# Where the expert units of the first batch begin: ahead of, or behind, the routing of its first part

## The chip, the cores and the metric

The kernel runs on one core of a Trainium2 chip. A core has a matrix engine (PE, TensorE), a vector engine (DVE, VectorE), a scalar engine (ACT, ScalarE), GpSimd (POOL) and a sync engine (SP) that issues most transfers. The metric is the time of one execution in device microseconds, and the median over runs counts.

## The reference

Four sequences of 10048 tokens with 128 channels go through an attention over 49 agents, and then through a two-level mixture of experts. Cut to what matters:

```
a2k   = softmax(scale * agents @ k.T)      # 49 x 10048, for each batch
agent_v = a2k @ v                          # 49 x 128
x     = softmax(scale * q @ agents.T) @ agent_v
g     = argmax(x @ w_group)                # 4 groups
e     = argmax(x @ w_expert[g])            # 4 experts in each
out   = p_g * p_e * (relu(x @ w1[g, e]) @ w2[g, e])
```

Every token goes to one of 16 experts (128 to 1024 to 128 channels), and its row is scaled by the two probabilities.

## The kernel before

The batches are taken in the order SEQ = (1, 2, 3, 0). For each of the first three, one expert is chosen (the one that most of its first tokens want), and all its tokens go through that expert; what belongs to others is counted and would be done at the end. The last batch is sorted by expert. A number in 32 bits is carried as a high and a low half in 16 bits (xh, xl; hh, hl), so most products on PE come in two or three matmuls.

Tokens go in tiles of 512 (20 for each batch). An own tile has 8 units: `first` (L1270) multiplies the tile's transposed weights et with 128 columns of the expert's weights wbuf into a PSUM tile ph, of which there are three, ACT makes hh from it and DVE hl (`evicted`, L1263); `second` (L1282) multiplies hh and hl with w2 into po, eight units behind (LAG). At the eighth unit of a tile `out_rows` scales po by oo and writes it out; oo is read by `factors` (L1314) from cwt, where `weigh` has written the tokens' weights.

All other work of a batch lies in lanes, generators that emit a few instructions at each step: q0 to q3 (queries: load, scores, exponentials, split into halves), k1 to k3 (keys and values, up to the agents' vectors), a0 to a3 (`followed`, L680: logits, routing, weights), p3 (sorting). A batch's lane a goes in parts of a few tiles; `skewed` (L284) runs stage two of a part beside stage one of the next. After each unit `advance` (L1479) steps lanes that are behind their due share (QUEUE), as long as a budget for DVE and ACT lasts, and an a lane at most twice. A step that yields a number of units rests for so long. `own_tile` (L1507) and `run_second` (L1519) step lanes until what they need is there: et and the weights, or the tokens' weights for the tile whose eighth unit is second in line.

What the program emits is a priority; the instructions of each engine are laid out when the kernel is compiled, in an order in which one whose inputs are there may come before one that was emitted earlier. On the chip each engine goes through its own queue in that order.

The opening (L1551 to L1568) does the keys, the values and the first queries of the first batch by itself. `agents_done` ends with the choice of the expert (`choose_first`, L590) and the loads of its w1 and w2, and steps q0 three times at each of its own. `part_logits` makes the logits of part one (tiles 0 and 1). `part_weights` (L803) then has three things for part one: `expert_split` at high priority (the product of the first weights with the agents' vectors, the split of w1 and w2 into halves), `routing` (L866), and `weigh` (L906) with the write of cwt. At its first yield the opening runs 14 rounds over q0, k1 and a0 (L1565 to L1568). Only behind all that come the units. While `wide` is on, that is in the opening, PSUM tiles of lanes are taken from all eight banks, afterwards from three.

Of the kernel before, what the change touches and what calls it, by code (L numbers as in the profile page):

```python
# [11 lines left out]
F16 = mybir.dt.float16  # L12
# [22 lines left out]
TQ = TS // P  # L35
# [24 lines left out]
SEQ = (1, 2, 3, 0)  # L60
NOWN = B - 1
SORTED = SEQ[NOWN]
# [3 lines left out]
PARTS = ((0, 2), (2, 5), *SORTS[1:])  # L66
ST = 5 * TQ
# [9 lines left out]
AHEAD_TURNS = 2  # L77
HOP = 2
LANDING = 7
OPENING = (3, 14)  # L80
LAG = 8
GROUP = 4
STRIP = P // GROUP
# [58 lines left out]
def build(ctx, tc, qT, kT, v, agT, wr, w1, w2, cpk, out, cols):  # L142
# [28 lines left out]
    def bank(any_=True):  # L171

        if wide[0] and any_:
            turns[0] += 1
            k = turns[0] % 8
            if k in (0, 3, 6):
                return ps1.tile([P, TS], F32, name="ph")
            if k in (1, 4):
                return ps2.tile([P, TQ, C], F32, name="po").rearrange("p a c -> p (a c)")
        return psa.tile([P, 512], F32, name="at", tag="at")  # L180
# [43 lines left out]
    wbuf = [const.tile([P, 2 * F], I32, name=f"wbuf{i}") for i in range(NB)]  # L224
# [9 lines left out]
    state = {b: {} for b in range(B)}  # L234
# [49 lines left out]
    def skewed(n, *stages):  # L284

        for i in range(n + len(stages) - 1):
            yield "chunk"
            live = [[stages[k](i - k), 0] for k in reversed(range(len(stages))) if 0 <= i - k < n]
            while live:
                moved = False  # L290
                for x in list(live):
                    if x[1] > clock[0] and not forced[0]:
                        continue
                    y = next(x[0], "end")
                    if y == 0:
                        continue
                    moved = True
                    if y == "end":
                        live.remove(x)
                        continue  # L300
                    if isinstance(y, int):
                        x[1] = clock[0] + y
                    yield
                if not moved:
                    yield 0
# [374 lines left out]
    def followed(b):  # L680

        parts = PARTS if b == SEQ[0] else SORTS
        first_part = 1 if b == SEQ[0] else 0
        moved = lambda f: lambda k: f(b, *parts[k + first_part])
        yield from skewed(len(parts) - first_part, *[moved(f) for f in ((part_logits, part_positions, part_rows) if b == SORTED else (part_logits, part_weights))])
        if b == SORTED:
            yield from order(b)

# [79 lines left out]
    def turned(b, i):  # L768

        n = min(TQ, NT - i * TQ)  # L770
        while b != SORTED and sum(len(state[o].get("et", {})) for o in SEQ[:NOWN]) >= ETB - 2:
            yield 0
        ptr = bank().bitcast(F16)
        r = i * TQ // ST
        for q in range(n):
            pe.transpose(ptr[0:2 * NA, q * P:(q + 1) * P], state[b]["rows", r][:, i * TQ + q - r * ST, 0:2 * NA], ident)
        et = ep.tile([2 * NA, TS], F16, name="es", bufs=2) if b == SORTED else ep.tile([2 * NA, TS], F16, name="et")
        act.activation(et[:, 0:n * P], ptr[0:2 * NA, 0:n * P], AF.Copy)
        state[b].setdefault("et", {})[i] = et
        state[b].setdefault("turned", set()).add(i)  # L780
        state[b].setdefault("all", {})[i] = et
        yield

    def ends(i0, i1):
        return i0 * TQ, NTP if i1 == OT else i1 * TQ

    def have(b, i):
        return ("split", (min(NT, (i + 1) * TQ) - 1) // CT) in state[b]

    def part_logits(b, i0, i1):  # L790

        st = state[b]
        for i in range(i0, i1):
            while not have(b, i):
                yield 0
            if b != SORTED and i not in st.setdefault("turned", set()):
                yield from turned(b, i)
        while "rh" not in st:
            yield 0
        yield HOP  # L800
        yield from logits(b, *ends(i0, i1))

    def part_weights(b, i0, i1):  # L803

        st = state[b]
        if "expert" in st and i0 == 0:
            st["weights"] = wbuf[SEQ.index(b)].bitcast(F16)
            with tc.high_priority():
                for _ in expert_split(b, st.pop("expert"), st["weights"]):
                    pass  # L810
            st["ready"] = True
            yield from routing(b, *ends(i0, i1))
            cnt = rt.tile([P, NE], F32, name=f"cnt{b}")
            vec.tensor_reduce(out=cnt, in_=st["oh"], axis=AX.X, op=ALU.add)
            st["cnts"] = [cnt]
        else:
            yield from routing(b, *ends(i0, i1))
            if i0 == 0:
                yield from choose(b)
                st["ready"] = True  # L820
        yield from weigh(b, *ends(i0, i1))
        yield
        st["weighed"] = i1
        yield from kept(b, *ends(i0, i1))
# [12 lines left out]
    def logits(b, t0, t1):  # L837

        st = state[b]
        NL = NG + NE + 1  # L840
        r0 = t0 // ST * ST
        if t0 == r0:
            st["lg", r0 // ST] = pc.tile([P, NL, ST], F32, name="lg")
            if NTP <= r0 + ST:
                vec.memset(st["lg", r0 // ST][:, :, NT - r0:], 1.0)
        z = min(NT, t1)
        i0, i1 = t0 // TQ, -(-z // TQ)
        if b == SORTED:
            yield from turned(b, i0)
        pl = bank()  # L850
        for i in range(i0, i1):
            if b == SORTED and i + 1 < i1:
                yield from turned(b, i + 1)
            elif b == SORTED:
                yield HOP
            et = st["all"].pop(i)
            for t in range(i * TQ, min((i + 1) * TQ, z)):
                o = pl[:, (t - t0) * NL:(t - t0 + 1) * NL]
                for h in range(2):
                    pe.matmul(o, et[:, (t - i * TQ) * P:(t - i * TQ + 1) * P], st["rh"][:, h], start=(h == 0), stop=(h == 1))  # L860
            yield HOP if i + 1 == i1 else None
        plv = pl[:, 0:(z - t0) * NL].rearrange("p (t g) -> p t g", g=NL)
        act.activation(st["lg", r0 // ST][:, :, t0 - r0:z - r0].rearrange("p g t -> p t g"), plv, AF.Copy)
        yield HOP
# [313 lines left out]
    def expert_split(b, x, ws):  # L1178

        w1f, w2f = x["w"]  # L1180
        for h in range(2):
            ps = bank()
            s = slice(h * 512, (h + 1) * 512)
            pe.matmul(ps, state[b]["at"], w1f[:, s], start=True, stop=True)
            yield HOP
            act.activation(ws[:, s], ps, AF.Copy)
            vec.tensor_sub(out=ws[:, F + h * 512:F + (h + 1) * 512], in0=ps, in1=ws[:, s])
            yield
        wv = ws[:, 2 * F:].rearrange("p (k h c) -> p k h c", k=FB, h=2)
        tc.keep_in_program_order(act.activation(wv[:, :, 0], w2f, AF.Copy, scale=W2S))  # L1190
        yield
        for h in range(2):
            z = slice(h * FB // 2, (h + 1) * FB // 2)
            vec.scalar_tensor_tensor(out=wv[:, z, 1], in0=w2f[:, z], scalar=W2S, in1=wv[:, z, 0], op0=ALU.mult, op1=ALU.subtract)
            yield
# [13 lines left out]
    def load_ahead(*which):  # L1209
        for x in which:  # L1210
            loaded[x] = load(*x)
# [292 lines left out]
    def lane(name):  # L1504
        return next(y for y in lanes if y["name"] == name)
# [39 lines left out]
    def along(n, *names):  # L1545
        clock[0] += 1
        for y in [lane(x) for x in names for _ in range(n)]:
            if y["until"] <= clock[0]:
                step(y)

    A = SEQ[0]  # L1551
    with tc.tile_pool(name="early", bufs=1) as early:
        qe = early_queries(A)
        for _ in front(A, early, ORDER, qe):
            pass
        for _ in qe:
            pass
        load_ahead(*[("q", A, 1 + i) for i in range(KA)], ("k", SEQ[1], 0))
        for _ in agents_done(A, early):
            along(OPENING[0], "q0")  # L1560
        for _ in part_logits(A, *PARTS[0]):
            clock[0] += 1
        resting = True
        for _ in part_weights(A, *PARTS[0]):
            if resting and "weights" in state[A]:  # L1565
                resting = False
                for _ in range(OPENING[1]):
                    along(1, "q0", "k1", "a0")  # L1568
    mo = ctx.enter_context(tc.tile_pool(name="mo", bufs=2))
    wide[0] = False  # L1570

# [88 lines left out]
```

## Time and profile before

| | |
|---|---|
| median of 3 runs | 937.5 us (936.94 to 937.96) |
| profiled execution | 937.08 us, its span 935.0 us |
| busy share of the span | PE 92%, DVE 80%, ACT 66%, POOL 50% |
| mean granted clock of PE | 0.974 of 2.4 GHz |

The span goes from the first to the last instruction of the profiled execution. A busy share is an average over stages that have different limits. The chain that ended last is followed back from the last instruction to whatever released each step; its shares say where the time of the whole was set. Instructions in the trace bear the line of a helper (L137 stands for nearly all of PE, DVE and ACT), so they are told apart by the tiles that they write and read. The granted clock is 0.5 when PE is held at 1.2 GHz and 1.0 at 2.4 GHz.

### The profile page before, as it was taken

How to read it: one execution, taken by the hardware profiler on the slowest of the kernel's cores; microseconds unless marked ns; L12 is line 12 of the kernel's file. 1: busy time of each engine (PE TensorE's matmuls, PEld its weight loads, DVE VectorE, ACT ScalarE, POOL GpSimd, SP SyncE). 2: the span in 40 equal slices, each digit the busy share in tenths (PEclk: the TensorE clock that was granted, in tenths of full speed). 3: DMA queues.
4: the chain of work that ended last, by engine and by line, in shares of the span. 5: the costliest groups of instructions: out<-in, count | busy, mean ns of one | idle time of the engine just before them, and what ended most of it. 6: DMA issues, size and time to landing. Idle time of an engine off the chain costs nothing.

```text
span 935.0 us, 22679 instructions
## 1 busy us (share of the span) xinstructions
PE 856.8 (92%) x8626; PEld 510.1 (55%) x8627; DVE 752.4 (80%) x1627; ACT 621.6 (66%) x1084; POOL 468.5 (50%) x618
## 2 busy tenths in 40 slices
PE   3878998999999899989799989999999999999996
PEld 2764554544555454544455545554444467787775
DVE  5647799898679898869988998989998766666673
ACT  4438787876878776767678867776656555555552
POOL 3146656653647343475647433556555405444545
PEclk9777999999999999999999999999999999999999
DMA  9656732746435554553635243233485435555442
GB/s 307 187 180 203 243 126 85 241 146 203 134 113 178 180 169 145 178 166 102 184 97 164 94 148 98 87 132 101 165 263 194 166 121 185 187 187 175 156 158 100
DMA packets 96495, 150.63 MB, mean 161 GB/s; under 512 B 8984, under 2 KB 61843, under 8 KB 96377
## 3 DMA queue, kind: packets, MB, share of 16 engines
q1 hardware_dynamic: 91225, 138.80, 46.6%
q0 software_dynamic: 5152, 10.30, 3.2%
q8 instruction: 69, 1.13, 0.5%
q14 instruction: 49, 0.40, 0.1%
HBM read 108.04 MB, written 39.69 MB: 158 GB/s over the span
## 4 chain that ended last, share of the span: by engine, by line
PE 49%; DVE 28%; DMA 6%; ACT 6%; POOL 6%; issue 5%; SPq 1%; POOLq 0%; ACTq 0%; DVEq 0%
PE po L137 25%; PE ph L137 14%; DVE hl L137 10%; PE at L137 10%; DVE vl L137 3%; POOL xl L273 3%; ACT hh L137 2%; DVE oh L137 2%; DVE oo L137 1%; DVE S L137 1%; DMA out<-oo,er 1%; DMA oo<-cwt 1%; DVE mq L137 1%; DVE rd L137 1%; DVE ef L137 1%
## 5 line engine op out<-in xcount | busy, mean ns | idle before, releaser
L137 DVE SCALAR_TENSOR_TENSOR hl<-ph,hh 128x512 f16<-128x512 f32 (+1 forms) x562 | 376.1, 676 | 121.3 <-ACT hh L137 117.2
L137 ACT ACTIVATE hh<-ph 128x512 f16<-128x512 f32 (+1 forms) x562 | 328.6, 592 | 190.2 <-PE ph L137 110.2
L137 PEld LDWEIGHTS <-wbuf 128*128 128x128 f16 (+2 forms) x2852 | 246.2, 98 | 294.2 <-issue 58.2
L137 PE MATMUL ph<-et,wbuf 98*128 98x512 f16 (+2 forms) x1048 | 318.8, 379 | 23.0 <-DVE hl L137 22.1
L137 PE MATMUL po<-hh,wbuf 128*128 128x512 f16 (+1 forms) x960 | 287.4, 378 | 0.9 <-DVE oo L137 0.9
L273 POOL TENSOR_TENSOR xl<-xf,xh 128x256 f16<-128x256 f32 x280 | 188.2, 707 | 150.3 <-ACT xh L137 133.9
L137 PE MATMUL po<-hl,wbuf 128*128 128x512 f16 (+1 forms) x480 | 181.2, 377 | 0.0
L1338 POOL DMA_INDIRECT out<-oo,er x82 | 80.5, 981 | 108.9 <-ACT hh L137 53.1
L137 PE MATMUL po<-wbuf,hh 128*128 128x128 f16 x1312 | 116.6, 219 | 0.0
L137 PE MATMUL po<-wbuf,hl 128*128 128x128 f16 x656 | 112.9, 219 | 0.0
L1065 POOL DMA_INDIRECT sorted_rows<-rows,slot x79 | 79.9, 1012 | 61.8 <-ACT hh L137 41.0
L137 PEld LDWEIGHTS <-hh 128*128 128x128 f16 x1312 | 99.2, 98 | 9.0 <-issue 9.0
L137 ACT ACTIVATE xh<-xf 128x1280 f16<-128x1280 f32 (+2 forms) x59 | 73.7, 1251 | 17.9 <-PE at L137 7.7
L760 POOL TENSOR_TENSOR rows<-ef,rows 128x245 f16<-128x245 f32 (+1 forms) x62 | 40.1, 668 | 62.3 <-ACT rows L137 62.3
L137 PEld LDWEIGHTS <-xh 128*128 128x128 f16 (+1 forms) x1164 | 58.0, 98 | 23.1 <-issue 5.5
L137 PEld LDWEIGHTS <-hl 128*128 128x128 f16 x656 | 64.2, 98 | 0.0
L480 POOL TENSOR_TENSOR sl<-S,sh 128x245 f16<-128x245 f32 (+2 forms) x51 | 35.8, 724 | 51.1 <-ACT sh L137 39.6
L137 PE MATMUL at<-agh,xl 128*128 128x49 f16 x543 | 54.4, 185 | 6.1 <-POOL xl L273 6.0
L137 DVE SCALAR_TENSOR_TENSOR hl<-at,hh 128x512 f16<-128x512 f32 x82 | 55.8, 681 | 0.0
L137 PE MATMUL at<-agh,xh 128*128 128x49 f16 x543 | 54.5, 185 | 1.2 <-DVE base L137 1.0
L137 PE MATMUL at<-agl,xh 128*128 128x49 f16 x543 | 54.2, 185 | 0.0
L137 PEld LDWEIGHTS <-xl 128*128 128x128 f16 x582 | 48.1, 98 | 8.5 <-POOL xl L273 8.1
(290 smaller groups left out, 1179.4 us busy)
## 6 DMA issues: line engine op xcount, KB each, us to landing
wbuf<-wdr SPq DMA_DIRECT2D x22, 832.0 KB
vf<-v SPq DMA_DIRECT2D x28, 640.0 KB
xf<-qT SPq DMA_DIRECT2D x28, 640.0 KB
cols<-oo SPq DMA_DIRECT2D x60, 256.0 KB
xf<-kT SPq DMA_DIRECT2D x23, 640.0 KB
oo<-cwt SPq DMA_DIRECT2D x57, 256.0 KB
erow<-rows SPq DMA_DIRECT2D x12, 490.0 KB
er<-sorted_rows SPq DMA_DIRECT2D x19, 256.0 KB
```

What stands on the lines that cost most here:

```text
L137: return f(*a, **k)
L273: pool.tensor_sub(out=xl[:, a:z], in0=xf[:, a:z], in1=xh[:, a:z])
L480: pool.tensor_sub(out=sl[0:m, y][:, z], in0=x[:, z], in1=sh[0:m, y][:, z])
L760: pool.tensor_sub(out=x0[:, a:z, NA:2 * NA], in0=ef[:, a:z], in1=x0[:, a:z, 0:NA])
L1065: ins = pool.indirect_dma_start(out=sorted_rows[:, :], out_offset=bass.IndirectOffsetOnAxis(ap=at, axis=0), in_=x, in_offset=None, bounds_ ...
L1338: ins = pool.indirect_dma_start(out=out, out_offset=bass.IndirectOffsetOnAxis(ap=to, axis=0), in_=y, in_offset=None, bounds_check=N - 1, o ...
```

## The change

The rounds over the lanes go out of the opening. Behind the logits of part one the opening now emits `expert_split` at high priority and marks the batch ready, and so the first units follow at once. Lane a0 starts with part one instead of part two: it passes over its logits, which are there, and does the routing, the counts and the weights of part one in its steps between the units. The amount of arithmetic is the same.

```diff
--- before.py
+++ after.py
@@ -77,7 +77,7 @@
 AHEAD_TURNS = 2
 HOP = 2
 LANDING = 7
-OPENING = (3, 14)
+OPENING = 3
 LAG = 8
 GROUP = 4
 STRIP = P // GROUP
@@ -680,9 +680,8 @@
     def followed(b):
 
         parts = PARTS if b == SEQ[0] else SORTS
-        first_part = 1 if b == SEQ[0] else 0
-        moved = lambda f: lambda k: f(b, *parts[k + first_part])
-        yield from skewed(len(parts) - first_part, *[moved(f) for f in ((part_logits, part_positions, part_rows) if b == SORTED else (part_logits, part_weights))])
+        moved = lambda f: lambda k: f(b, *parts[k])
+        yield from skewed(len(parts), *[moved(f) for f in ((part_logits, part_positions, part_rows) if b == SORTED else (part_logits, part_weights))])
         if b == SORTED:
             yield from order(b)
 
@@ -790,6 +789,9 @@
     def part_logits(b, i0, i1):
 
         st = state[b]
+        if ("lg", i0 * TQ // ST) in st and i0 == 0:
+            yield
+            return
         for i in range(i0, i1):
             while not have(b, i):
                 yield 0
@@ -803,12 +805,7 @@
     def part_weights(b, i0, i1):
 
         st = state[b]
-        if "expert" in st and i0 == 0:
-            st["weights"] = wbuf[SEQ.index(b)].bitcast(F16)
-            with tc.high_priority():
-                for _ in expert_split(b, st.pop("expert"), st["weights"]):
-                    pass
-            st["ready"] = True
+        if b == SEQ[0] and i0 == 0:
             yield from routing(b, *ends(i0, i1))
             cnt = rt.tile([P, NE], F32, name=f"cnt{b}")
             vec.tensor_reduce(out=cnt, in_=st["oh"], axis=AX.X, op=ALU.add)
@@ -1557,15 +1554,14 @@
             pass
         load_ahead(*[("q", A, 1 + i) for i in range(KA)], ("k", SEQ[1], 0))
         for _ in agents_done(A, early):
-            along(OPENING[0], "q0")
+            along(OPENING, "q0")
         for _ in part_logits(A, *PARTS[0]):
             clock[0] += 1
-        resting = True
-        for _ in part_weights(A, *PARTS[0]):
-            if resting and "weights" in state[A]:
-                resting = False
-                for _ in range(OPENING[1]):
-                    along(1, "q0", "k1", "a0")
+        state[A]["weights"] = wbuf[SEQ.index(A)].bitcast(F16)
+        with tc.high_priority():
+            for _ in expert_split(A, state[A].pop("expert"), state[A]["weights"]):
+                pass
+        state[A]["ready"] = True
     mo = ctx.enter_context(tc.tile_pool(name="mo", bufs=2))
     wide[0] = False
```

## Rows read from the trace of the kernel before

**Rows 1.** The page: busy time of each engine; the chain that ended last, by engine.
```profile
span 935.0 us, 22679 instructions
...
PE 856.8 (92%) x8626; PEld 510.1 (55%) x8627; DVE 752.4 (80%) x1627; ACT 621.6 (66%) x1084; POOL 468.5 (50%) x618
...
PE 49%; DVE 28%; DMA 6%; ACT 6%; POOL 6%; issue 5%; SPq 1%; POOLq 0%; ACTq 0%; DVEq 0%
```
**Rows 2.** Stretches: us, busy of PE, PEld, DVE, ACT, POOL; PEclk, DMA share, GB/s.
```profile
64.40:68.75 4.35, 2.85 (x5) 1.22 (x5) 3.47 (x22) 1.39 (x4) 0.00 (x0) 0.50 1.03 321
69.45:81.10 11.65, 8.71 (x128) 5.71 (x127) 5.57 (x13) 8.16 (x14) 6.31 (x10) 0.65 0.84 285
81.10:98.10 17.00, 16.20 (x119) 7.54 (x118) 16.94 (x42) 14.74 (x24) 12.74 (x20) 0.91 0.49 159
98.10:126.00 27.90, 27.89 (x278) 15.13 (x278) 21.02 (x39) 20.29 (x35) 12.15 (x20) 1.00 0.67 218
```
**Rows 3.** The same view, finer, around the first units.
```profile
69.60:74.30 4.70, 3.29 (x90) 3.05 (x89) 3.56 (x7) 4.27 (x6) 0.90 (x2) 0.86 0.99 374
74.30:79.40 5.10, 3.57 (x31) 1.88 (x30) 1.90 (x3) 3.26 (x7) 5.10 (x9) 0.50 0.61 195
74.30:84.50 10.20, 8.67 (x48) 3.83 (x47) 5.30 (x13) 6.21 (x11) 7.62 (x13) 0.51 0.63 206
```
**Rows 4.** The chain in order of time: start, us, what.
```profile
62.50 3.44 DMA w1f<-w
...
79.58 0.87 PE ph L137 x2
```
**Rows 5.** Timeline of PE: start, us, instruction, idle before it and its releaser.
```profile
67.85 1.91 PE L137 MATMUL at<-w1f,at 128*128 128x512 f32 x2
...
74.33 1.91 PE L137 MATMUL ph<-et,wbuf 98*128 98x512 f16 x4
...
77.26 0.22 PE L137 MATMUL at<-agh,xl 128*128 128x49 f16 x1 [0.94 <-POOL xl L273]
...
77.89 0.22 PE L137 MATMUL at<-agh,xl 128*128 128x49 f16 x1 [0.20 <-POOL xl L273]
```
**Rows 6.** Timeline of DVE.
```profile
64.45 0.24 DVE L137 TENSOR_TENSOR oh<-lg 128x80 f16<-128x80 f32 x1 [1.32 <-ACT lg L137]
...
68.79 0.69 DVE L137 TENSOR_TENSOR wbuf<-ph,wbuf 128x512 f16<-128x512 f32 x1 [0.18 <-ACT wbuf L137]
...
70.50 0.69 DVE L137 TENSOR_TENSOR wbuf<-at,wbuf 128x512 f16<-128x512 f32 x1 [0.94 <-ACT wbuf L137]
...
73.69 0.41 DVE L137 TENSOR_SCALAR cw<-rs,scb 128x8 f32<-128x8 f32 x1
...
76.58 1.29 DVE L137 SCALAR_TENSOR_TENSOR hl<-ph,hh 128x512 f16<-128x512 f32 x2
81.10 0.69 DVE L137 SCALAR_TENSOR_TENSOR hl<-ph,hh 128x512 f16<-128x512 f32 x1 [3.22 <-ACT hh L137]
...
96.70 0.62 DVE L137 TENSOR_TENSOR oo<-po,oo 128x512 f32<-128x512 f32 x1
97.25 0.71 DVE L137 TENSOR_SCALAR cw<-rs,scb 128x12 f32<-128x12 f32 x1
```
**Rows 7.** Timeline of ACT.
```profile
54.18 1.27 ACT L137 ACTIVATE xh<-xf 128x1280 f16<-128x1280 f32 x1 [2.24 <-DMA xf<-kT]
...
70.30 1.05 ACT L137 ACTIVATE wbuf<-w2f 128x1024 f16<-128x1024 f32 x1
...
75.98 1.05 ACT L137 ACTIVATE hh<-ph 128x512 f16<-128x512 f32 x2
```
**Rows 8.** Timeline of SP's queue of transfers.
```profile
76.10 0.35 SPq L959 DMA_DIRECT2D cwt<-cwc  x1
...
77.42 0.34 SPq L1318 DMA_DIRECT2D oo<-cwt  x1
...
104.97 0.81 SPq L1318 DMA_DIRECT2D oo<-cwt  x2
```

## The prediction

> **What bounds the kernel now.** Read first the share of each engine and the shares of the chain that ended last: TensorE (PE) is busy 92% of 935.0 us and holds 49% of the chain, VectorE (DVE) 28% [rows 1]. That is an average; the change touches the place where the opening turns into the stream of expert units, so the second view is the table of windows around it [rows 2]. It shows three regimes. From 64.40 to 68.75 the weights of the first expert are under way and DVE works 22 small instructions, the routing and weighing of part one, in 3.47 us of 4.35. From 69.45 to 81.10 no engine is full: DVE 5.57 of 11.65 us, so 6.08 us idle, PE 8.71, at a granted clock of 0.65. From 81.10 to 98.10 DVE is busy 16.94 of 17.00 us, and behind that PE 27.89 of 27.90. What is lost in the second regime is paid for afterwards by a DVE, then a PE, that has no hole left. So the question is how much of that regime the change fills.
>
> Third view, the timelines of the engines there. The load of the weights is on the chain for 3.44 us from 62.50 [rows 4]. PE finishes the product of the weights at 69.76 (67.85 + 1.91) [rows 5], DVE finishes the low half of the first 512 features at 69.48 (68.79 + 0.69) [rows 6]. With that the first four units have all they need: the turned tiles 0 and 1 were made in the opening. Yet the first unit starts on PE at 74.33, four matmuls for two units, and the third only at 79.58 [rows 4, 5]. In between PE takes scores of later chunks of queries and keys, and waits in them for GpSimd's low halves: 0.94 us once and about 0.20 three times [rows 5]. DVE gets its first two hl at 76.58 and the third at 81.10 after 3.22 us of nothing [rows 6].
>
> **The change part by part.** (a) The 14 rounds over the lanes q0, k1 and a0, up to 42 steps, go out of the opening. In program order the first units now stand right behind the split of the weights, ahead of the scores that PE took from 69.56 to 79.40. (b) Routing, weighing and the transposed weights of part one move from ahead of the units into lane a0, which gives at most two steps per unit.
>
> Program order is not engine order, and the trace says so. The first keys of the second batch (xh at 54.18 [rows 7]) are issued in the code by the 14 rounds, behind the split of the weights, and ran 14 us ahead of it. Likewise DVE began the routing at 64.45, ahead of its first weight instruction at 68.79 [rows 6], though the code has the weights first. So what has its inputs fills holes from behind, and program order decides only between instructions that could all run. I take (b) to cost nothing for that reason: the 22 instructions still find DVE idle until 68.79, since the tile of logits that they read is made before the weights in either kernel. If that cover is gone, they cost their 3.47 us [rows 2] in a stretch where DVE is full.
>
> Gain of (a), counted on DVE, which sets the end of the next regime. Available: 6.08 us [rows 2]. Not regained:
> - 0.94 us before 70.50 [rows 6]. ACT must first make the second half of the weights and then w2 (70.30 + 1.05, so 71.35 [rows 7]); no hh, and so no hl, exists before.
> - The ring of three PSUM tiles. At the lower clock one unit takes 0.87 us on PE (two matmuls [rows 4]), about 0.6 on ACT (1.05 for two [rows 7] overlapped, so an estimate between 0.53 and 0.6) and 0.69 on DVE [rows 6]: 2.16 us for three units, 0.72 each, where DVE alone takes 0.64 (1.29 for two [rows 6]). 0.08 us for each of the eight units before the second products start: 0.64 us.
> - The three short waits for GpSimd, 0.59 us. It makes a low half of 256 columns in more time than PE uses it, in whatever order. The long wait of 0.94 goes: PE came to those scores 0.1 us after the units ran out, and now has units between.
>
> 6.08 - 0.94 - 0.64 - 0.59 = 3.91 us. The bounds: if the clock stays up and the ring costs nothing, 5.1; if PE stands in scores for the whole 1.53 us and the two long waits of DVE shrink to half only, 2.1.
>
> What is moved by (a) beside that: DVE's share of the 42 steps is small and in the 5.57 us already. SP's loads of later chunks leave later; DMA is full there (0.99 at 374 GB/s from 69.60 to 74.30 [rows 3]), and the query chunk among them (the fourth) is wanted no earlier than tile 7, unit 56, so I cost it at nothing, between minus 0.5 and plus 0.5 us (w2 may land a little earlier, a key chunk later). GpSimd's subtractions move from a stretch with 6.31 of 11.65 us busy to one with 12.74 of 17.00 [rows 2]: still room. (b) also sends two transfers past SP's queue, the write of the weights of part one and the broadcast read, now at 76.10 and 77.42 [rows 8]; the first output product is at 96.70 [rows 6], 19 us later, so 4 us less leaves room.
>
> The clock. From 74.30 to 84.50 the granted clock is 0.51, from 69.60 to 74.30 it is 0.86 [rows 3]: PE, idle for 1.41 us of the second (4.70 - 3.29), rose to 2.4 GHz within it and then ran the first units at 1.2 GHz. Units that follow at 69.76 close that pause, but the three PSUM tiles can open another, so the sum has the lower clock for all eight units.
> The Trainium skill (TensorE: Matmul & The Clock Gate, Part 1: The HAM clock gate) says that the throttled state is the default and activity releases it; by it the 8.67 us of PE work from 74.30 to 84.50 would take half, the ring would cost nothing and the gain would be the upper bound. The trace agrees as far as one rise and one fall show.
>
> **Sum.** The profiled execution took 937.08 us (span 935.0 and 2.1 around it); 937.08 - 3.91 = 933.2. It lies 0.4 below the median of the runs, 937.5, so the same sum against the median gives 933.6, which I forecast. Later regimes are tied to units and not to the clock on the wall, so I see nothing that takes a shift back, except the rivals.
>
> **Rivals.** First, no change: the 42 steps were filling holes, and what fills them no longer is owed later. PE's work from 69.60 to 74.30 is 3.29 us at 0.86 and, from 74.30 to 79.40, 3.57 at 0.50 [rows 3], of which the units are 1.91 [rows 5], so 1.66: 2.83 + 0.83 = 3.7 us at full clock. From 98.10 on PE is full [rows 2], so work that drops out of the holes comes back one for one: 3.9 - 3.7 leaves 0.2 us, 937.3. For it: that PE stretch. Against: the early start of the keys at 54.18, which shows that the steps fill holes wherever they are emitted. The same time comes out if the scheduled order hardly changes, so that the edit does not do what it says.
>
> Second, slower: the weights of part one come too late for the first output. If lane a0 is not drawn forward, the routing's 3.47 us fall into full DVE and take nearly all of the gain. Then the factors hang on the lane's last steps, which the code forces at the latest before the eighth second product, at the sixteenth unit. In part two the way from cw (97.25) to the read of its factors (104.97) took 7.7 us [rows 6, 8], in part one 3.7 (73.69 to 77.42). With cw among the units at about 91 the read goes out between 94.7 and 98.7, and the product that wants it would be due at 92.8 (96.70 - 3.9): a wait of 1.9 to 5.9, say 4 us, in which every hl behind the product stands too. 0.4 us of gain less 4: 941.1. It decides from the place of cw: later than about 85 us and the product waits. For it: two steps per unit and the lane's own pauses. Against: again the 22 instructions that ran early.
> The Trainium skill (TensorE: Matmul & The Clock Gate, Architectural detail) has VectorE as a strict FIFO; by it one product that waits for a transfer holds the whole engine. DVE's 3.22 us ahead of one hl do not show the contrary; no row shows it held by a transfer.
>
> **How the numbers follow.** The forecast, 931.4 to 935.4 (gain 6.1 to 2.1), has 0.57; no change, 936 to 939, has 0.23; the late weights, 939 to 943, 0.20. The likeliest case's own range is the first pair. For 8 in 10 I need the forecast and the case of no change, with a little of the third: 931.2 to 939.5. A measurement of this kernel tells 0.2%, 1.9 us, from nothing. Faster by more than that: 0.57; within: 0.22; slower: 0.21.
>
> **What would show it.** In the changed profile the first ph<-et,wbuf should stand at 69.7 to 70.5, the third unit's hl before 76, DVE idle between 69.45 and the start of its full stretch under 3 us, and the read of the first factors before 85. The routing should still begin near 64.5; if it is found among the hl, the second rival is at work. If PE idles or stays at 1.2 GHz up to 84, or the units start early and the 98 us mark is reached no earlier, the forecast is wrong at (a).

## The result, and the profile after

Over five runs each, the changed kernel takes 942.52 us (941.06 to 944.18), the kernel before 937.50 beside it (936.94 to 939.83): ratio 1.0054, 95% interval 1.0033 to 1.0075. It is slower by 5 us, where 933.6 was forecast and 931.2 to 939.5 was the range. The profiled execution took 944.18 us (span 942.3).

The page of the changed kernel: span, busy time of each engine, the chain by engine. The chain's share of DMA has gone from 6% to 8% [rows 1].

```profile
span 942.3 us, 22670 instructions
...
PE 858.5 (91%) x8626; PEld 510.0 (54%) x8627; DVE 749.8 (80%) x1627; ACT 621.7 (66%) x1084; POOL 468.7 (50%) x618
...
PE 48%; DVE 25%; DMA 8%; ACT 7%; POOL 6%; issue 5%; SPq 1%; POOLq 0%; ACTq 0%; DVEq 0%
```

Stretches of the changed kernel, the columns as in [rows 2].

```profile
69.45:81.10 11.65, 10.10 (x105) 5.26 (x104) 8.93 (x18) 9.66 (x16) 6.11 (x10) 0.93 0.73 277
81.10:98.10 17.00, 13.65 (x165) 7.93 (x164) 8.25 (x15) 12.31 (x20) 12.34 (x21) 1.00 0.83 242
98.10:126.00 27.90, 26.99 (x262) 14.31 (x261) 24.12 (x60) 20.73 (x37) 12.37 (x20) 0.94 0.51 160
...
74.30:79.40 5.10, 4.18 (x45) 2.27 (x44) 3.22 (x7) 4.02 (x7) 4.41 (x8) 1.00 0.43 148
```

The stretch that was to be filled is filled: DVE works 8.93 of 11.65 us, where it worked 5.57 [rows 2], and the clock is 1.00 from 74.30 to 79.40, where it was 0.50 [rows 3]. The next one, in which DVE was to be full, has it at 8.25 of 17.00 us. What ended that idleness stands on the timeline of DVE:

```profile
64.95 0.24 DVE L137 TENSOR_TENSOR oh<-lg 128x80 f16<-128x80 f32 x1 [1.17 <-ACT lg L137]
...
71.59 0.22 DVE L137 TENSOR_SCALAR cw<-rs,scb 128x8 f32<-128x8 f32 x1
...
73.12 1.88 DVE L137 SCALAR_TENSOR_TENSOR hl<-ph,hh 128x512 f16<-128x512 f32 x3
...
91.28 0.67 DVE L137 TENSOR_TENSOR most<-at,most 128x490 f32<-128x490 f32 x1 [2.07 <-ACT S L137]
96.27 0.69 DVE L137 TENSOR_TENSOR oo<-po,oo 128x512 f32<-128x512 f32 x1 [4.32 <-DMA oo<-cwt]
96.88 1.28 DVE L137 SCALAR_TENSOR_TENSOR hl<-ph,hh 128x512 f16<-128x512 f32 x2
```

The units start 3.5 us earlier than in [rows 6] (73.12 against 76.58), and at the fifteenth hl they are 8.2 us ahead (87.05 against 95.29). The first output product, however, stands at 96.27, where it stood at 96.70: DVE waits 4.32 us in front of it for the weights of part one, and the hl behind it waits too. The timeline of PE and the chain in order of time (start, us, what) tell where these weights were:

```profile
84.22 0.27 PE L137 MATMUL at<-cp,cw 128*8 128x128 f32 x1
...
97.61 0.59 PE L137 MATMUL ph<-et,wbuf 98*128 98x512 f16 x2 [3.08 <-DVE hl L137]
```
```profile
86.20 4.21 DMA cwt<-cwc
90.48 5.76 DMA oo<-cwt
...
118.93 3.47 DMA cwt<-cwc
122.41 4.34 DMA oo<-cwt
```

The weights (cw) are computed at 71.59. Their transposition comes 12.6 us later, then a trip through memory: 4.21 us until the write has landed, 5.76 us for the read. The third product (126.77) waits 1.69 us for part two's weights in the same way.

### The profile page after: what moved, and what is told of

It reads as the page before. It is cut to its first block, busy times and chain, and to the rows that moved or that the text cites. A ratio compares the mean times of both kernels' runs of the same rounds, so it can differ in the third digit from the quotient of the medians.

```text
span 942.3 us, 22670 instructions
## 1 busy us (share of the span) xinstructions
PE 858.5 (91%) x8626; PEld 510.0 (54%) x8627; DVE 749.8 (80%) x1627; ACT 621.7 (66%) x1084; POOL 468.7 (50%) x618
## 4 chain that ended last, share of the span: by engine, by line
PE 48%; DVE 25%; DMA 8%; ACT 7%; POOL 6%; issue 5%; SPq 1%; POOLq 0%; ACTq 0%; DVEq 0%
PE po L137 25%; PE ph L137 13%; PE at L137 9%; DVE hl L137 9%; POOL xl L273 4%; DVE vl L137 3%; ACT hh L137 2%; DMA oo<-cwt 2%; DVE oh L137 1%; DVE oo L137 1%; DVE S L137 1%; DMA cwt<-cwc 1%; DMA out<-oo,er 1%; ACT vh L137 1%; DVE mq L137 1%
## 5 line engine op out<-in xcount | busy, mean ns | idle before, releaser
L137 DVE SCALAR_TENSOR_TENSOR vl<-vf,vh 128x640 f16<-128x640 f32 (+2 forms) x51 | 48.5, 963 | 6.3 <-ACT vh L137 6.2
```

Source lines behind the costliest of these rows:

```text
L137: return f(*a, **k)
```

## The experiments

All ratios are to runs of the kernel before on the same chip, beside the kernel in question; a pair of numbers in brackets is the 95% interval. The first twelve had it at 937.5 to 938.3 us, the last six at 942.6 to 943.0, so times of different comparisons are set side by side by ratio only. The theories: **W**, the trip of part one's weights through memory holds DVE; **O**, lane work not done in the opening is owed later; **J**, the chain from queries to part two's weights is emitted just in time; **S**, steps of q0 put PE into scores that wait for GpSimd; and the last, which the traces gave, **P**, routing runs beside GpSimd and is slowed by it.

**The rounds alone** (first half of the change; the kernel before without its 14 rounds):

```diff
         for _ in part_weights(A, *PARTS[0]):
-            if resting and "weights" in state[A]:
...
-                    along(1, "q0", "k1", "a0")
+            pass
```


> The first half of the change alone: the 14 rounds go, but routing and weights of part one are still emitted in the opening, ahead of the first units. Theory W (the round trip of part one's weights, written at 86.2 us and read back at 90.5 to 96.2 in the changed kernel, holds VectorE at the first output product and takes back the lead of 8.2 us that the units had): the trip starts near 75 us here, nobody waits for it, and the time is 932 to 936 us. Theory O (the 14 rounds filled holes, and their lane work is owed later whatever waits): 937 to 940 us, the units lead early and have no lead left by 130 us.

939.32 us, 1.0021 (0.9998 to 1.0044), where O had it (937 to 940). Nothing waits at the first product (at 89.37 in its profile), yet the kernel is not faster.

**The wait taken away.** Part one's transposition, copy and write at high priority in the changed kernel:

```diff
...
+            soon = tc.high_priority() if b == SEQ[0] and t0 == 0 else nullcontext()
+            with soon:
...
+                sync.dma_start(out=cwt[SEQ.index(b)][t0:t1], in_=ct[0:n])
```


> The changed kernel, with the transpose, the copy and the write of part one's weights at high priority; nothing else moves by hand. W: the write goes out some 5 us or more earlier, the wait at the first output product (4.3 us on VectorE, 3.1 us on TensorE) goes for the most part, 935 to 938 us. O: the wait goes but the time stays at 940 us or above, since the same work is still to be done.

940.56, 1.0041 (1.0023 to 1.0058), where O had it (940 or above) and not W; the write is issued at 79.57, and the first product stands at 88.34 with no wait.

The next two read rows of v in place of the tokens' weights, for tiles 0 and 1, and for tiles 0 to 4:

```diff
+        there = v[x["b"], t:t + n] if x["b"] == SEQ[0] and x["own"] < 2 else cwt[SEQ.index(x["b"])][t:t + n]
...
```


> The changed kernel, but the factors of tiles 0 and 1 of the first batch are read from the input v instead of the written weights, so the first two output products hang on no round trip (their values are not the weights). W: 942.5 less about 7 us, 934 to 937 us. O: less than a third of the 7 us comes back, 940 us or above.

> As the kernel without the trip for tiles 0 and 1, and for tiles 2 to 4 too, whose weights are written at 118.9 us and waited for until 126.8 in the changed kernel. W: some 2 us below the kernel without the trip for tiles 0 and 1, 932 to 935 us. O: no different from it.

939.80, 1.0032 (1.0016 to 1.0049), and 939.55, 1.0022 (1.0007 to 1.0037). W had forecast 934 to 937 and 932 to 935. By the medians, then, the first wait is worth 1 to 3 of the 5 us and the second at most 1; 2 to 4 us remain, against 2 with the rounds alone. The intervals overlap with that of the changed kernel (1.0033 to 1.0075), so these sizes are not clear of noise.

**Which rounds.** The kernel before with its 14 rounds over fewer lanes:

```diff
-                    along(1, "q0", "k1", "a0")
+                    along(1, "k1")
```


> The kernel before, with the 14 rounds over k1 alone (no q0, no a0). The first four experiments showed that with all round trips of tiles 0 to 4 taken away some 2 us stay lost. Theory J (just in time: without the rounds the query lane q0 gets no step in the first 16 units, the split of its second chunk is emitted only when tile 2 asks for it at the 17th unit, and the logits, routing and weights of part two follow late, so units stand still between 95 and 127 us): this kernel emits them as late, 939 to 942 us, though it keeps the rounds of the keys. Theory O (the work of the keys that no longer fills holes is owed later): it keeps that work in the holes, 936 to 938.5 us.

> The kernel before, with the 14 rounds over q0 alone. J: the split of the second chunk is emitted ahead of the units and part two's weights at the 25th unit, six ahead of their need; 934 to 938 us. O: the keys' work is owed, 939 to 942 us.

> The kernel before, with the 14 rounds over q0 and a0 (no k1). J: everything that tiles 2 to 4 wait for is emitted as in the kernel before, and units give way to fewer scores of keys: 933 to 937.5 us. O: 939 to 942 us, as for the rounds over q0 alone.

With the keys only it is 939.49, 1.0026 (1.0006 to 1.0046), as without rounds: J had it so, and the rounds of the keys by themselves are worth nothing. With the queries only it is 942.95, 1.0068 (1.0053 to 1.0084), against J. With queries and parts it is 937.24, 1.0004 (0.9986 to 1.0023), as in the kernel before and as J had it. For the queries only, the windows (columns as above) and one of five such rows of PE show S:

```profile
74.50:79.50 5.00, 2.45 (x30) 1.28 (x28) 1.89 (x4) 4.67 (x9) 5.00 (x9) 0.85 0.37 105
79.50:84.50 5.00, 4.80 (x42) 2.22 (x40) 1.80 (x4) 1.84 (x4) 3.37 (x6) 0.50 0.78 228
```
```profile
77.28 0.20 PE L137 MATMUL at<-agh,xl 128*128 128x49 f16 x1 [1.80 <-POOL xl L273]
```

PE stands in scores until GpSimd has made the low halves, its granted clock is 0.50 (1.2 GHz) in the second stretch, and DVE has 3.69 us of work in 10.

Two more tries to advance the queries: the 14 rounds over q0 behind the weights of the kernel with the early write, and the chain to the turned tiles 2 to 4 in the rounds' place, in the kernel before:

```diff
+        for _ in range(14):
+            along(1, "q0")
```


> The changed kernel with both suspected causes taken away: the transpose, copy and write of part one's weights at high priority, and 14 rounds over q0 alone between the split of the weights and the first unit. J: 934 to 938 us, some 5 us or more below the changed kernel. O: 940 us or above.

```diff
...
+        while ("split", 1) not in state[A]:
+            along(1, "q0")
+        while 4 not in state[A]["turned"]:
+            along(1, "a0")
```


> The rounds go, part one's weights stay in the opening (as in the first experiment), and then q0 is stepped only until its second chunk is split and a0 only until the tiles 2 to 4 are transposed; then the units. Against the first experiment (939.3 us) this adds nothing but J's chain. J: 934 to 937 us. S: 939 us or above.

941.43, 1.0054 (1.0034 to 1.0074), and 941.17, 1.0029 (1.0007 to 1.0051): two misses for J. The next tests early writes as such, all parts' weights at high priority in the kernel before (the edit of the early write without its condition):

> The kernel before with the transpose, copy and write of every part's weights at high priority. The trip of part three (write at 164.2 us, output product at 171.9 after 1.2 us of waiting) is there in both kernels. If the trips' tails are late only by their place in the order: 934 to 937 us. If they follow the weights themselves, which are computed at 163.2: no difference, 936.5 to 938.5 us.

942.89, 1.0056 (1.0037 to 1.0074): slower, and no theory had said so; not explained.

**How many rounds.** The kernel before with 7 over all lanes, 7 over q0 and a0, 4 and 10:

```diff
-OPENING = (3, 14)
+OPENING = (3, 7)
```


> The kernel before with 7 rounds over q0, k1 and a0 instead of 14. Seven is where the split of the second query chunk is emitted. J (part two's chain must be emitted early; more rounds are not needed): 935 to 938 us. Theory S (each step of q0 in the opening puts TensorE into scores that wait for GpSimd, as in the kernel with 14 rounds over q0 alone, where VectorE worked 1.8 to 2.5 of each 5 us from 74.5 to 89.5): fewer such steps help, 934 to 937 us, but the rounds over q0 and a0 alone would be slower than these.

> The kernel before with 7 rounds over q0 and a0, none over k1. J: the chain of tiles 2 to 4 is emitted 15 units ahead of its need, the third chunk's scores are not, units start near 70 us: 933 to 936.5 us. S: 938 to 943 us, as with 14 rounds over q0 alone.

> The kernel before with 4 rounds over q0, k1 and a0 instead of 14 (14 gave 937.5 us, 7 gave 933.5, none 939.3). In the order that the program emits, with 4 rounds the split of the second chunk of queries and the weights of part two fall to the last unit that may force them (the factors of tile 2 are made at the very unit that wants them), as with none. J (the chain to part two's weights must be emitted ahead of the units; where it is made just in time the lead of the units is given back): 938.5 to 941, and the third output product waits for its factors. Rival D (every round less is worth the same, and the keys' and agents' steps count alike): between 7 and none, 935 to 937.

> The kernel before with 10 rounds instead of 14. The second chunk of queries is split and the weights of part two are made as far ahead of their unit as with 7 or 14 rounds. J: units start a little earlier than with 14 and nothing is owed, so between 933.5 (7) and 937.5 (14): 934 to 937. Rival C (the 933.5 of 7 rounds is how its instructions happen to fall, no rule of lead): 937 to 939, same as before.

With 7 rounds it is 933.50, 0.9953 (0.9937 to 0.9970); with 7 without k1 937.41, 1.0001 (0.9986 to 1.0016), between what J and S had. With 4 the ratio is 0.9962 (0.9935 to 0.9990; 939.24 us beside 942.98), with 10 it is 1.0021 (0.9993 to 1.0049), against J and as rival C had it, by which the gain of 7 is how its instructions happen to fall. With 4 rounds part two's chain is emitted as late as with none, and its product waits 2.05 us as J said, yet its ratio lies below that of none (1.0021) as of 14 (1). So a late chain does not by itself make the kernel slower, and J alone is not the cause.

**The second half alone, and on 7 rounds.** The changed kernel with 14 or 7 rounds:

```diff
         state[A]["ready"] = True
+        for _ in range(14):
+            along(1, "q0", "k1", "a0")
```


> The changed kernel with the 14 rounds kept behind the split of the first weights: the second half of the change alone, the routing and weights of part one in lane a0. They are emitted three units ahead of the first output product. W: the trip of 8 to 10 us starts about five units before it is wanted, so a wait of 0 to 3 us at that product, 937 to 940. Rival (the half costs nothing by itself, as the prediction's step b had it): 937 to 938, no wait.

> The changed kernel with 7 rounds over q0, k1 and a0 behind the split of the first weights. Against the 7 rounds at 933.5 it differs only in that the routing and weights of part one stand in lane a0, where they are emitted just in time for the first output (at the unit that wants them). W (the round trip of part one's weights through memory, when it starts that late, holds VectorE at the first output product): a wait of 1 to 5 us ahead of that product and 936 to 940. Rival (the place of part one's weights costs nothing where the queries are advanced): 933 to 935 and no wait.

With 14 rounds it is 0.9992 (0.9964 to 1.0019), with no wait: with units that start late the trip is covered, and the second half by itself costs nothing. With 7 it is 1.0008 (0.9980 to 1.0035), with a wait of 1.51 us at the first product, against 0.9953 where part one's weights stay in the opening. So their place costs there, as W has it, but the ratios differ by some 5 us, more than the wait.

**Beside GpSimd.** What is different between 4 rounds and none stands on DVE's timeline, in the routing of part two. First the kernel that has no trip (its timelines of DVE and of GpSimd):

```profile
98.26 0.83 DVE L137 TENSOR_TENSOR oh<-lg 128x120 f16<-128x120 f32 x1
99.01 0.75 DVE L137 TENSOR_TENSOR rm<-lg 128x120 f32<-128x120 f32 x1
99.68 0.64 DVE L137 TENSOR_SCALAR zz<-lg 128x12 f32<-128x12 f32 x1
...
100.97 0.62 DVE L137 TENSOR_TENSOR gm<-rm 128x12 f32<-128x12 f32 x1
101.52 0.21 DVE L137 RECIPROCAL zr<-zz 128x12 f32<-128x12 f32 x1
...
102.16 0.68 DVE L137 SCALAR_TENSOR_TENSOR hl<-ph,hh 128x512 f16<-128x512 f32 x1
...
105.34 0.67 DVE L137 TENSOR_TENSOR oo<-po,oo 128x512 f32<-128x512 f32 x1
```
```profile
94.50 6.47 POOL L273 TENSOR_TENSOR xl<-xf,xh 128x256 f16<-128x256 f32 x10 [1.97 <-ACT xh L137]
100.93 1.22 POOL L759 TENSOR_TENSOR rows<-ef,rows 128x245 f16<-128x245 f32 x2
102.11 2.83 POOL L273 TENSOR_TENSOR xl<-xf,xh 128x256 f16<-128x256 f32 x5
```

Then DVE in the kernel with 4 rounds (GpSimd idle between 97.28 and 99.52):

```profile
97.28 0.27 DVE L137 TENSOR_TENSOR rm<-lg 128x120 f32<-128x120 f32 x1
97.47 0.16 DVE L137 TENSOR_SCALAR zz<-lg 128x12 f32<-128x12 f32 x1
...
97.85 0.16 DVE L137 TENSOR_TENSOR gm<-rm 128x12 f32<-128x12 f32 x1
97.93 0.22 DVE L137 RECIPROCAL zr<-zz 128x12 f32<-128x12 f32 x1
```

The same rm takes 0.75 beside GpSimd's subtractions and 0.27 alone, zz 0.64 and 0.16, gm 0.62 (beside the subtraction of rows) and 0.16; a reciprocal (0.21) and an hl (0.68), which has one operand in PSUM, are the same. The Trainium skill (SBUF — State Buffer, Who interferes with whom) says that VectorE and GpSimd share one pair of ports to SBUF, taken for whole instructions: a VectorE instruction with two SBUF inputs contends with a GpSimd instruction that reads SBUF, and not with one that only writes; of one-input instructions it names tensor_scalar, as zz is, among those that can take the pair. These rows agree in which instructions suffer.

The test: the low halves of the last three key chunks of batch two are filled with zeros by GpSimd in place of being computed, in the kernel with no trip, and as a control in the kernel before.

```diff
...
+                if early is None and kind == "k" and b == SEQ[1] and ci > 4:
+                    pool.memset(xl[:, a:z], 0.0)
+                else:
+                    pool.tensor_sub(out=xl[:, a:z], in0=xf[:, a:z], in1=xh[:, a:z])
```


> The changed kernel without the trip of part one's weights (first output products read v), in which the same 15 subtractions of GpSimd are fills (the same low halves left out). In e4_no_trip part two's routing lay from 98.3 to 112.6 us beside those subtractions: 12 of its instructions took 7.15 us, 0.60 each, where alone they take about 0.2, and TensorE stood in that stretch. P: these instructions fall to 0.2 to 0.3 each, VectorE's full stretch shrinks by 3 to 5 us, the lead of the units at the first output product is kept, and the kernel is 2 to 5 us below the kernel before (ratio 0.995 to 0.998) and as far below its control. Rival J (part two's chain is emitted too late, whoever runs beside it): it stays at 1.002 to 1.003 of the kernel before, like e4_no_trip, with the instructions short.

> The control for the next kernel: the kernel before, in which the low halves of the last three chunks of the second batch's keys are set to zero by GpSimd instead of being computed (15 subtractions of two operands in memory become 15 fills, some 7 us less of GpSimd between 96 and 110 us; those keys' low halves are left out of the result). P (VectorE's small instructions of routing and weighing last two to four times as long beside GpSimd's subtractions): in the kernel before the routing of part two runs up to 97 us and is interleaved with the units while TensorE is full, so 0 to 2 us less than before. Without P: within 1 us of before.

With the fills the kernel with no trip is at 0.9972 (0.9947 to 0.9998), as P had it, where with the subtractions it had 1.0032 (1.0016 to 1.0049); the control is at 1.0001 (0.9980 to 1.0023). The same stretch of DVE, without the subtractions:

```profile
97.91 0.27 DVE L137 TENSOR_TENSOR oh<-lg 128x120 f16<-128x120 f32 x1
98.10 0.28 DVE L137 TENSOR_TENSOR rm<-lg 128x120 f32<-128x120 f32 x1
98.30 0.17 DVE L137 TENSOR_SCALAR zz<-lg 128x12 f32<-128x12 f32 x1
...
100.26 0.25 DVE L137 TENSOR_TENSOR oh<-oh 128x192 f16<-128x192 f16 x1
...
100.96 0.68 DVE L137 TENSOR_TENSOR oo<-po,oo 128x512 f32<-128x512 f32 x1
```

and of GpSimd, where fills run beside the oh at 100.26 and leave it short:

```profile
92.86 2.58 POOL L274 MEMSET xl<- 128x256 f16 x10 [0.67 <-PE at L137]
...
100.08 1.16 POOL L274 MEMSET xl<- 128x256 f16 x5
```

Not every overlap makes an instruction long: an oh of 120 columns at 98.90 took 0.16 here, though GpSimd's subtraction of rows stands from 98.84 to 100.13 in this trace.

From the first oh to the product it is 3.05 us (100.96 - 97.91) instead of 7.08 (105.34 - 98.26). The windows of the two, with the subtractions and then with the fills, say what the 4 us do to PE:

```profile
100.00:105.00 5.00, 2.99 (x27) 1.43 (x26) 5.00 (x11) 2.63 (x5) 4.94 (x9) 1.00 0.64 204
105.00:110.00 5.00, 3.33 (x23) 1.66 (x23) 4.90 (x15) 0.60 (x1) 0.00 (x0) 0.72 0.58 182
```
```profile
100.00:105.00 5.00, 5.00 (x56) 2.73 (x55) 4.99 (x15) 3.35 (x7) 1.24 (x6) 1.00 0.62 159
105.00:110.00 5.00, 5.00 (x77) 3.16 (x74) 4.50 (x15) 4.03 (x8) 2.35 (x4) 1.00 0.13 49
```

DVE is nearly full in both; with the short routing PE is full too, with the long one it stands for 3.7 of 10 us, and its granted clock in the second stretch is 0.72. The fills also make low halves sooner, but PE did not wait for a low half there. Both its waits with the subtractions were for DVE:

```profile
102.89 0.59 PE L137 MATMUL ph<-et,wbuf 98*128 98x512 f16 x2 [1.51 <-DVE hl L137]
...
106.67 0.59 PE L137 MATMUL ph<-et,wbuf 98*128 98x512 f16 x2 [2.16 <-DVE hl L137]
```

So P is shown for this kernel: beside those subtractions it loses some 0.6%. That P sets it apart from the kernel before is not shown, for that kernel pays too. Its routing of part two stands beside other subtractions of GpSimd (among them 82.30 to 85.48 and 88.62 to 95.27), and seven of its instructions are long. Three of these on DVE's timeline:

```profile
82.97 0.65 DVE L137 TENSOR_TENSOR gm<-rm 128x12 f32<-128x12 f32 x1
...
84.86 0.70 DVE L137 TENSOR_TENSOR oh<-oh,rc 128x120 f16<-128x120 f16 x1
...
93.98 0.71 DVE L137 TENSOR_TENSOR rs<-rh 128x24 f32<-128x24 f32 x1
```

All of DVE's instructions for routing and weighing part two take 8.8 us together in the kernel before, 10.0 with no trip, 5.7 with no trip and the fills, 6.5 with 4 rounds and 6.6 in the changed kernel. With no trip they are thus only 1.3 us longer than before; but there thirteen stand in a row with one hl among them, where the kernel before has its hl in between. The control's fills begin at 94.95, when nearly all of its routing is done. So no run takes the slowing out of the kernel before, and a part of what the fills and the 4 rounds gain may be no more than that.

The same in starts of the output products, less those of the kernel before (us, one profiled execution each). DVE's first instruction for the weights stands 0.5 us later than before in the changed kernel and 0.5 to 1.1 us earlier in the other three; the executions with no trip and with 4 rounds are the fastest and the second fastest of their runs:

```
product   before   after    no trip   no trip, fills   4 rounds
first      96.70   -0.43     -8.59       -8.94          -8.70
second    106.42   +0.82     -1.08       -5.46          -6.19
third     118.68   +8.09     +7.33       +2.25          +1.05
fifth     139.82   +1.98     +1.21       -3.87          -5.06
```

The lead of 8 us is lost ahead of the first product by the wait or, with no trip, between the first and the second. There 7.5 us go, and with the fills 3.5 still go: a first half of part two's routing stands in that place (3.05 us with the fills, one hl among them), which the kernel before has done ahead of its first product. So this part of the lead is work owed, as O has it, though it is routing and not the keys; the other 4.0 us go with the subtractions. With the fills and with 4 rounds about half of the lead lasts to the fifth product.

## Why the prediction was wrong

**Right.** The prediction had the view and the place right: the first ph stands at 70.04 (forecast 69.7 to 70.5), the third unit's hl before 76, the routing near 64.5 (64.95) and its cw at 71.59, so the 22 instructions did cost nothing. The clock did better than the sum had it: 0.83 from 69.60 to 74.30, in which PE worked 4.08 of 4.70 us, then 1.00 to 79.40, and the time went the other way all the same. The rise is as the Trainium skill's rule (TensorE: Matmul & The Clock Gate, Part 1: The HAM clock gate) would have it.

**Wrong: step (b).** "the first output product is at 96.70 [rows 6], 19 us later, so 4 us less leaves room." Two things failed in it. The transfers did not keep their places: what fills holes from behind is work with ready inputs, but the transposition behind cw stood in the lane's last steps, and it came at 84.22, the write at 86.20 and the read at 90.48, where they were at 76.10 and 77.42 [rows 8]. And the trip was taken as short, from the kernel before, where the read left 1.3 us behind the write: here it took 4.21 + 5.76 = 9.97 us. The read "before 85" was the mark that the prediction itself gave, and it was missed by 5.5 us. Step (b) fails only on top of (a): with the 14 rounds kept it does cost nothing (0.9992).

So the second rival happened, in its place and by its mechanism: the wait was 4.32 us against 1.9 to 5.9, the time 942.5 against 941.1. One condition of it was wrong: it decided by the place of cw (later than 85 us), and cw was early; what was late came behind it. That its numbers come so near is in part luck. Its read leaves at 94.7 to 98.7 and costs nothing on the way, where the read left at 90.48 and took 5.76 us; and it has all of the loss in the wait, where taking the wait away returned 1 to 3 us. VectorE does hold its order behind a transfer, which the prediction had left open: one product kept the whole engine for 4.32 us. This is as the Trainium skill (TensorE: Matmul & The Clock Gate, Architectural detail) has it.

**Wrong: step (a) in its value.** "Later regimes are tied to units and not to the clock on the wall, so I see nothing that takes a shift back, except the rivals." The gain of 3.91 us did not come with (a) alone (1.0021 with the rounds gone), nor without the wait (1.0032 and 1.0022 with no trips). The prediction's own sign of this came too: the units start early, and the products of 96.70 and 106.42 come at 96.27 and 107.24. What the runs show in its place has two parts. A part of the lead is the routing of part two put off, which comes back behind the first product; so the first rival, work owed later, was right in part, though not for the keys, whose rounds by themselves are worth nothing. And this routing then stands in a row beside GpSimd's subtractions, and its instructions last two to four times as long. The trace of before had shown that size: cw of 12 columns took 0.71 us and cw of 8 took 0.41 [rows 6]; the latter takes 0.22 at 71.59 in the changed kernel, and the former 0.23 at 107.59 in the kernel with the fills. How much of the missing gain each part is stays open, since the kernel before pays for slow routing as well.

Two of its bounds were also wrongly added: the 5.1 leaves out the three short waits (4.6 with them), and the 6.1 of the range is the whole idle time, of which step (a) itself says that some can't be regained. The time came out beyond the other end, so neither decides.

In the changed kernel itself few long instructions appear (rx, 0.85 at 106.21; cw, 0.71 at 113.86), as GpSimd has a pause where the routing begins. Its GpSimd, then its DVE:

```profile
100.54 3.19 POOL L273 TENSOR_TENSOR xl<-xf,xh 128x256 f16<-128x256 f32 x5 [1.85 <-ACT xh L137]
104.69 1.23 POOL L759 TENSOR_TENSOR rows<-ef,rows 128x245 f16<-128x245 f32 x2 [0.96 <-ACT rows L137]
```
```profile
103.84 0.27 DVE L137 TENSOR_TENSOR rm<-lg 128x120 f32<-128x120 f32 x1
```

So the two costs don't add: with the wait there is little slowing, and whoever takes the wait away gets the slowing. That fits the 1 to 3 us that came back without the wait, and the 0.9972 without both.

**Left open.** Of the 7.3 us that the changed kernel's span is longer in the profiled execution, 2.0 are lost by the fifth product and 4.8 by the eighth (187.11 against 182.30), where the order of instructions is the same as before. In the chain there:

```profile
166.17 3.67 DMA cwt<-cwc
169.85 5.16 DMA oo<-cwt
...
175.79 5.08 PE po L137 x15
```

Before, these took 2.97, 4.72 and 3.40: a longer trip, behind which PE ran at a lower clock (0.83 from 172 to 182, where it was 1.00). No run tells whether that belongs to the change or to this execution. The 7 rounds have the best ratio, but their profiled execution, the slowest of their eight (937.56 us), shows no lead at the fifth product (+1.36), so their gain is not explained, nor that it goes without the keys (1.0001); nor is the loss of that gain with 10 rounds, or the slower time with all early writes. To delay GpSimd's or VectorE's instructions without leaving any out was not tried.

Two versions beat both kernels: 7 rounds (0.9953, 0.9937 to 0.9970) and 4 rounds (0.9962, 0.9935 to 0.9990), with part one's weights in the opening. In the trace of the second the lead is seen to last.

## What to carry to other kernels

When work is moved into slots between others, follow it to its last instruction and price its whole trip from issue to use; that its first instructions ran early says nothing of its tail. And when work starts earlier, ask what runs on the neighbour engine at its new time: a stretch that is full in both kernels can be full of longer instructions, so compare the duration of the same instruction, not only the busy share, and count in the kernel before what it already pays.

## What the hardware showed that was not expected

- A write of part one's weights and the read of them for the first tiles, on the same queue of SP, took 4.21 and 5.76 us to land while the DMA engines were busy for most of the stretch (0.83 from 81.10 to 98.10).
- VectorE's zz (12 columns) and rm (120 columns), with operands in SBUF, went from 0.16 to 0.64 us and from 0.27 to 0.75 beside GpSimd's subtractions; beside its fills of the same tiles an oh of 192 columns took 0.25, where it had 0.75 beside the subtractions at 104.02.
- The units started 3.5 us earlier, with TensorE at a granted clock of 1.00 (2.4 GHz) in place of 0.50 from 74.30 to 79.40, and the kernel was slower by 5 us.
